# A filter layer by DFT products and a snake MLP in one kernel: a first stage folded on GpSimd for batches 3 to 7, and the sign of the filter put into its copy

## The chip, the core and the metric

The kernel runs on one core of a Trainium2 chip. The time is device time in microseconds, from several runs of one program; the profile is of one further execution. The engines are TensorE (PE, its weight loads shown as PEld), VectorE (DVE), ScalarE (ACT), GpSimd (POOL) and SyncE (SP, which here issues transfers only). TensorE writes to PSUM; ACT and DVE move results from there to SBUF.

## The reference

Two layers follow each other. The first multiplies the spectrum of `x` along the sequence by a filter; the second is an MLP with a snake activation.

```python
# x (8, 3008, 256); filt_r, filt_i (1505, 256)
X = np.fft.rfft(x, axis=1)
y = np.fft.irfft(X * (filt_r + 1j * filt_i)[None], n=3008, axis=1)
h = y.reshape(24064, 256) @ w_in              # (256, 2048)
s = np.sin(alpha * h)
g = h + s * s / (alpha + 1e-9)
out = g @ w_out                               # (2048, 256), float32
```

## The kernel before

The DFT of length 3008 = 47 x 64 is done in two stages of matrix products. The first (`first`, tile `pa`) is a DFT of length 47: 94 rows (47 positions, twice, for two halves of the 64 columns) against the table `wf_t`, 16 products of 512 columns a batch, each evacuated by `evac` into `t1_h` and stored four at a time to `d1` in DRAM. `load_t2` reads `d1` back with other rows (eight transfers on POOL's queue, two for each of four groups `t2[g]`). `forward` (`pb`, 12 a batch) is the second stage. `product` and `cross` multiply by the filter on DVE; for `cross`, SP swaps the two halves of `xf` into `xs`. `inverse` (`pc`) and `last` (`pd`) go back, by way of `d2` in DRAM and `load_t4` (tile `t_a`), and leave the rows in `y`. Batch 0 has functions of its own, with names ending in `_0`.

The MLP takes `y` in 48 chunks of 512 columns (the sixth of each twelve has 384). `hidden` makes 128 of the 2048 hidden rows (two products `ph`), ACT takes a sine of it, DVE forms the activation `v` with one operation on `cos_all` (SBUF) and `ph` (PSUM); `project` multiplies by `w_out` (`po`), ACT copies the result to `o`, and `store` issues it, on POOL's queue for chunks below 5, and on SP's after.

The order of the work is written out by hand. The main loop goes through 8 steps a chunk; a step has two `hidden`, a `slot`, one or more `project`, and another `slot`. Work of the filter layer stands in the list `pending`, put there with a place in steps (`put`); `slot(at)` takes from it what is due, at most one piece with TensorE work unless one is over a step late. For a batch b the places count from z = 48 b. Before, in batches 3 to 7, `load_x` stands at z - 92 + 7 ch, `first` at z - 67 + 0.66 i, `load_t2` at z - 56, `forward` from z - 46.8 every 2.3 steps, `product` and `cross` 1.5 and 4.5 steps after it, `inverse` 6 after, `load_t4` at z - 10.5 and z - 3. Each engine works through its own instructions in this order, and so do the queues that SP and POOL issue. On SP stand the stores to `d1` and `d2`, the swaps, `load_t4`, and from chunk 5 the stores of `o`.

The filter's two parts lie in `f_t[0]` and `f_t[1]`, each wanted in both halves of the partitions. `other_half` copies one half into the other; `negate`, at steps 13 and 14, turns the sign of half of `f_t[1]` in place. Batch 0 works before that, and has the missing sign in its own table, `e1_0`, through the vector `sign`.

Of the kernel before, what the change touches and what calls it, by code (L numbers as in the profile page):

```python
# [22 lines left out]
NR = 2 * N1  # L23
NK = 4 * NS
FUSED = 1


def dft_tables():

    n1, n2 = np.arange(N1), np.arange(N2)  # L30
    s, q = np.arange(NS), np.arange(NQ)
    ph = 2 * np.pi * np.outer(n1, s) / N1
    w = np.stack([np.cos(ph), -np.sin(ph)], 1)
    wf = np.zeros((N1, 2, 2, NS, 2))
# [12 lines left out]
    d[0, :, :, 0] = c.transpose(0, 2, 1)
    d[1, :, :, 0] = sn.transpose(0, 2, 1)
    d[0, :, :, 1] = (-sn * sg).transpose(0, 2, 1)
    d[1, :, :, 1] = (c * sg).transpose(0, 2, 1)  # L50
    f16 = np.float16
    wf, wi = wf.reshape(N1 * 2, 2, NS, 2), 2 * wi.reshape(2, NS, 2, NR)
    wf0, wi0 = np.zeros((96, 2, 2, 32)), np.zeros((2, 2, 32, NR))
    wf0[:NR, :, :, :NS] = wf.transpose(0, 1, 3, 2)
    wi0[:, :, :NS] = wi.transpose(0, 2, 1, 3)
    d = d.reshape(128, NS, 128).astype(f16)
    e = d.transpose(2, 1, 0) * f16(0.125)
    return (wf.reshape(NR, NK).astype(f16), wi.reshape(NK, NR).astype(f16), d,
            wf0.reshape(96, 128).astype(f16), wi0.reshape(128, NR).astype(f16), e)


# [1 line left out]
def kernel(  # L63
# [8 lines left out]
    out: bass.AP,  # L72
):
    nc = tc.nc
    wf_host, wi_host, d_host, wf0_host, wi0_host, e_host = dft_tables()
    wf_dram = nc.inline_tensor(wf_host, name="wf_tbl")
    wi_dram = nc.inline_tensor(wi_host, name="wi_tbl")
    d_dram = nc.inline_tensor(d_host, name="d_tbl")
    wf0_dram = nc.inline_tensor(wf0_host, name="wf0_tbl")
    wi0_dram = nc.inline_tensor(wi0_host, name="wi0_tbl")  # L80
# [13 lines left out]
        return ctx.enter_context(tc.tile_pool(name=name, bufs=bufs, **kw))  # L94

    cpool = pool("consts", 1)
    xpool = pool("xp", 4)
    t2pool = pool("t2", 4)
    xfpool = pool("xf", 3)
    ppool = pool("pp", 4)  # L100
# [7 lines left out]
    ops = pool("ops", 2, PSUM)  # L108

    wf_t = cpool.tile([NR, NK], FP16)  # L110
    t1_h = [cpool.tile([128, 16, C], FP16, name=f"t1_h{i}") for i in range(2)]
    t4_a = cpool.tile([128, 2, 16, C], FP16)
    t4_h = [t4_a[:, i] for i in range(2)]

    def by_half(t):

        return t.rearrange("p a (b c) -> p (a b) c", c=128)

    cos_all = cpool.tile([128, 4, 512], FP32)
    y = cpool.tile([128, 2, 2, 32, NR], FP16)  # L120
# [15 lines left out]
    marks = {}  # L136

    def load_x(b, ch):
        xt = xpool.tile([NR, 8, C], FP16, name=f"x_{b}_{ch}", tag="x")
        for n0, n in [(0, 8)] if b or ch < 3 else [(0, 4), (4, 4)]:  # L140
            ins = nc.gpsimd.dma_start(  # L141
                out=xt[:, n0:n0 + n],
                in_=bass.AP(tensor=x.tensor, offset=x.offset + (b * S + ch * 8 + n0) * C,
                            ap=[[32 * C, NR], [C, n], [1, C]]),
            )
        if b == 0:
            marks["x", ch] = ins
        if b == 1:
            marks["x1", ch] = ins
            after(ins, marks["w_out"])  # L150
        if b > 1:
            after(ins, marks["snake"])
        return xt
# [3 lines left out]
    def evac(dst, src, on_act=None):  # L157
# [3 lines left out]
        else:  # L161
            marks["dve"] = nc.vector.tensor_copy(out=dst, in_=src)  # L162

    class Spectral:

        def __init__(self, b):
            self.b = b
            self.d1 = dpool.tile([2 * NS, N2, C], FP16, name=f"d1_{b}", tag="d1")
            self.d2 = dpool.tile([2 * NS, N2, C], FP16, name=f"d2_{b}", tag="d2")
            self.d1_rows = self.d1.rearrange("a (h n) c -> (a h) n c", h=2)  # L170
            self.d2_rows = self.d2.rearrange("a (h n) c -> (a h) n c", h=2)
            self.x, self.t2, self.t4, self.xf, self.xs, self.p = {}, {}, {}, {}, {}, {}
            self.fused = b >= FUSED

        def load_x(self, ch):
# [2 lines left out]
        def first(self, i):  # L178
            ch, j = divmod(i, 4)
            ps = fps.tile([128, 512], FP32, name=f"pa_{self.b}_{i}", tag="f")  # L180
            marks["pe"] = nc.tensor.matmul(out=ps[0:NK, :], lhsT=wf_t, rhs=self.x[ch][:, 2 * j:2 * j + 2, :],  # L181
                                           start=True, stop=True)
            r0 = 8 * (ch % 2)
            evac(t1_h[ch // 2][0:NK, r0 + 2 * j:r0 + 2 * j + 2, :], ps[0:NK, :])
            if j == 3:
                nc.sync.dma_start(out=self.d1_rows[:, 8 * ch:8 * ch + 8, :], 
                                  in_=t1_h[ch // 2][0:NK, r0:r0 + 8, :])

        def load_t2(self, g):
            self.t2[g] = t2pool.tile([128, 6, C], FP16, name=f"t2_{self.b}_{g}", tag="t2")  # L190
# [73 lines left out]
    id32 = cpool.tile([16, 16], FP32)  # L264
    nc.scalar.dma_start(out=id32, in_=id32_dram.ap())

    x0 = [xpool.tile([NR, 8, C], FP16, name="x_0_0", tag="x")] + [load_x(0, ch) for ch in range(1, 4)]
    nc.gpsimd.dma_start(out=d_t, in_=d_dram.ap())
    id16 = cpool.tile([128, 128], FP16)
    nc.gpsimd.dma_start(out=id16, in_=id16_dram.ap())  # L270
# [86 lines left out]
        nc.tensor.transpose(out=ps[:, 0:16], in_=rec, identity=id32)  # L357
        nc.vector.tensor_scalar(out=rec_t, in0=ps[:, 0:16], scalar1=-0.5, scalar2=None, op0=ALU.mult)

    sign = cpool.tile([128, 1], FP32)  # L360
    nc.vector.memset(sign[0:64], 0.125)
    nc.vector.memset(sign[64:128], -0.125)

    def inverse_table(g):

        gs = slice(8 * g, 8 * g + 8)
        ps = ops.tile([128, 8, 128], FP16, name=f"pse_{g}", tag="o")
        for i in range(8):
            for a in range(2):
                nc.tensor.transpose(out=ps[64 * a:64 * a + 64, i, :],  # L370
                                    in_=d_t[:, 8 * g + i, 64 - 64 * a:128 - 64 * a], identity=id16)
        nc.scalar.mul(e1_0[:, gs, :], ps, sign)

    warmed = []

# [7 lines left out]
    def other_half(g, k, on_act):  # L383

        gs = slice(12 * g, 12 * g + 12)
        evac(f_t[k][64 - 64 * k:128 - 64 * k, gs, :], f_t[k][64 * k:64 * k + 64, gs, :], on_act)

    warm_pe(10)
    def cast_x0(h):
# [47 lines left out]

    def product_0(i):
        hc, w = blocks[i]
        p0[i] = xpool.tile([128, 2, 4, 128], FP16, name=f"p_0_{i}", tag="x")  # L440
        marks["products"] = nc.vector.tensor_tensor(
            out=p0[i].rearrange("p f s (k c) -> p f s k c", k=2),
            in0=xf0[i].rearrange("p s (k c) -> p s k c", k=2)[:, None].to_broadcast([128, 2, 4, 2, 64]),
            in1=filt_t[:, :, 4 * w:4 * w + 4].rearrange("p f s (k c) -> p f s k c", k=2)[..., 64 * hc:64 * hc + 64],
            op=ALU.mult)
# [24 lines left out]
            after(ins, marks["filt", 1, 0])  # L470
    nc.sync.dma_start(out=wf_t, in_=wf_dram.ap())
    nc.sync.dma_start(out=wi_t, in_=wi_dram.ap())
    w_out32 = vpool.tile([128, 16, C], FP32, name="w_out32", tag="v")
    for jb in range(0, 16, 8):
        ins = nc.sync.dma_start(out=w_out32[:, jb:jb + 8],
# [121 lines left out]
    for jb in range(12, 16):  # L597
        put(5 + 0.5 * (jb - 12), weights_out, jb, 1)

    def negate(i):  # L600

        gs = slice(12 * i, 12 * i + 12)
        nc.vector.tensor_scalar(out=f_t[1][0:64, gs, :], in0=f_t[1][0:64, gs, :],
                                scalar1=-1.0, scalar2=None, op0=ALU.mult)

    for i in range(2):
        put(13 + i, negate, i)
    for n0, n, at in ((6, 5, 1.5), (11, 4, 12.5), (15, 4, 14), (19, 4, 15.5), (23, 4, 17), (27, 5, 19)):
        put(at, last_0, n0, n, fps, "f", True)
    for b in range(1, B):  # L610
        s = s1 if b == 1 else Spectral(b)
        z = 48 * b
        if b > 1:
            for ch in range(4):
                put((22,27,32,37)[ch] if b == 2 else z - 92 + 7 * ch, s.load_x, ch)
        for i in range(16):
            put(6.9 + 0.35 * i if b == 1 else 36 + 0.66 * i if b == 2 else z - 67 + 0.66 * i, s.first, i, pe=True)
        for g in range(4):
            put(12.5 if b == 1 else max(z - 56, 46.5), s.load_t2, g)
        for u in range(12):  # L620
            inv = 23.5 + 1.25 * u if b == 1 else 59 + 2.1 * u if b == 2 else z - 40.8 + 2.3 * u
            fwd = inv - (6 if b == 1 else 6)
            put(fwd, s.forward, u, pe=True)
            put(fwd + (0.5 if b == 1 else 1.5), s.product, u)
            if s.fused:
                put(fwd + (4 if b == 1 else 4.5), s.cross, u)
            put(inv, s.inverse, u, pe=True)
        for ch in range(4):
            put(z - (9.5 if b == 1 and ch < 3 else (10.5, 10.5, 10.5, 3)[ch]), s.load_t4, ch)
        for u in range(16):  # L630
            put(z + (u - (5 if b == 1 else 6.5) if u < 4 else 2 * u - 9), s.last, u, pe=True)
# [59 lines left out]
```

## Time and profile before

| what | value |
|---|---|
| median of 3 runs | 785.87 us (785.68 to 786.81) |
| the profiled execution: its time, its span | 785.97 us, 784.2 us |
| granted TensorE clock | 0.999 |
| first-stage products (line 181) | 112 of 94x512, 42.4 us of pipelined busy time |
| activation on DVE (line 546) | 704 of 128x512, 682 ns each |
| transfers, share of 16 engines | hardware queue q1 33.4%, software queue q0 (POOL) 19.4% |

Busy time is the time in which an engine has at least one instruction under way. Matmuls overlap, so their lengths add to more than the time that they take; what one costs is read from the distance of starts. A line in a table of groups gives the source line, the engine, what is written and read, the shape, how often, the busy time, and the mean length; after the second bar stands the engine's idle time just ahead of these instructions, with what ended it. The span begins with the program's first instruction and ends with its last.

### The profile page before, as it was taken

What the parts mean: (1) busy time and instruction counts of PE and PEld (TensorE: products, weight loads), DVE (VectorE), ACT (ScalarE), POOL (GpSimd) and SP (SyncE); (2) the same over time, 40 slices, a digit from 0 to 9 for tenths busy, and PEclk for the clock granted to TensorE, in tenths of its full rate; (3) what the DMA queues carried; (4) which work ended last, traced back from release to release, by engine and by line L of the source; (5) the groups of instructions that cost most, each with busy time, mean ns of one, the idle gap of its engine ahead of it and who ended that gap; (6) DMA issues with size and microseconds to landing.
All of it is one profiled execution on the core that took longest, in us unless ns stands there. A gap on an engine that the chain in (4) does not pass through costs nothing.

```text
span 784.2 us, 16646 instructions
## 1 busy us (share of the span) xinstructions
PE 771.1 (98%) x5799; PEld 535.2 (68%) x5799; DVE 655.7 (84%) x1169; ACT 617.6 (79%) x1211; POOL 113.3 (14%) x190
## 2 busy tenths in 40 slices
PE   7999999999999999999999999999999999999998
PEld 4757766676667766777666766767667776766666
DVE  7897996899878997799877998799977999777773
ACT  5797987888878887888877887788887887777674
POOL 6456443500020000200020000200002000000000
PEclk9999999999999999999999999999999999999999
DMA  9956577755564546654575454835556243421112
GB/s 214 281 112 164 124 142 213 158 124 121 163 174 89 129 105 190 148 122 108 131 202 114 103 115 131 226 87 118 119 161 176 65 98 80 117 61 29 41 41 54
DMA packets 86655, 100.99 MB, mean 129 GB/s; under 512 B 14896, under 2 KB 74294, under 8 KB 86572
## 3 DMA queue, kind: packets, MB, share of 16 engines
q1 hardware_dynamic: 74644, 71.11, 33.4%
q0 software_dynamic: 11712, 28.78, 19.4%
q8 instruction: 45, 0.74, 0.4%
q14 instruction: 38, 0.31, 0.1%
q10 hardware_dynamic: 216, 0.05, 0.0%
HBM read 55.72 MB, written 46.66 MB: 131 GB/s over the span
## 4 chain that ended last, share of the span: by engine, by line
PE 92%; DVE 3%; DMA 1%; ACT 1%; issue 1%; SPq 0%; ACTq 0%; DVEq 0%
PE po L558 40%; PE ph L541 39%; PE pa L181 3%; PE pd L254 2%; PE pb L201 2%; PE pc L232 2%; DVE v L546 2%; PE pc L453 1%; DMA al<-in_moe_alpha_dram 1%; ACT cos_all L545 1%; PE warm L381 1%; PE pb L431 1%; DMA t_a<-d 0%; SPq L586 0%; PE pa L399 0%
## 5 line engine op out<-in xcount | busy, mean ns | idle before, releaser
L546 DVE SCALAR_TENSOR_TENSOR v<-cos_all,ph 128x512 f16<-128x512 f32 (+1 forms) x768 | 482.9, 671 | 106.8 <-ACT cos_all L545 103.6
L545 ACT ACTIVATE cos_all<-ph 128x512 f32<-128x512 f32 (+1 forms) x768 | 411.2, 592 | 95.3 <-PE ph L541 94.3
L558 PE MATMUL po<-w,v 128*128 128x256 f16 x3008 | 389.5, 272 | 0.0
L541 PE MATMUL ph<-y,w 128*128 128x512 f16 (+1 forms) x1536 | 387.8, 374 | 1.6 <-DVE y L162 0.9
L558 PEld LDWEIGHTS <-v 128*128 128x128 f16 x3008 | 288.3, 98 | 78.3 <-issue 2.0
L541 PEld LDWEIGHTS <-w 128*128 128x128 f16 x1536 | 147.9, 98 | 103.9 <-issue 3.1
L566 ACT COPY o<-po 128x512 f32<-128x512 f32 (+1 forms) x97 | 55.6, 573 | 19.9 <-PE po L558 13.5
L586 POOL DMA_DIRECT2D out_dram<-o x67 | 35.0, 529 | 207.6 <-ACT o L566 205.4
L193 POOL DMA_DIRECT2D t<-d x56 | 36.3, 664 | 180.4 <-DMA out_dram<-o 98.7
L204 ACT CAST xf<-pb 128x512 f16<-128x512 f32 x84 | 50.0, 595 | 13.1 <-PE pb L201 12.3
L141 POOL DMA_DIRECT2D x<-in_x_dram x32 | 17.1, 537 | 259.7 <-PE pc L232 146.5
L160 ACT CAST t_h<-pa 96x512 f16<-96x512 f32 x74 | 43.3, 585 | 8.8 <-PE pa L181 8.5
L160 ACT CAST y<-pd 128x376 f16<-128x376 f32 (+1 forms) x82 | 39.5, 482 | 8.8 <-PE pd L254 5.3
L254 PEld LDWEIGHTS <-t_a 96*128 96x128 f16 x448 | 31.3, 97 | 19.8 <-DMA t_a<-d 1.4
L181 PE MATMUL pa<-x,wf_t 94*96 94x512 f16 x112 | 42.4, 381 | 0.6 <-ACT t_h L160 0.4
L160 ACT CAST g<-pc 128x512 f16<-128x512 f32 x61 | 36.2, 593 | 8.2 <-PE pc L232 7.8
L254 PE MATMUL pd<-wi_t,t_a 96*128 96x94 f16 x448 | 37.1, 204 | 1.1 <-DMA t_a<-d 1.1
L222 DVE TENSOR_TENSOR p<-p,xs 128x512 f16<-128x512 f16 x84 | 35.7, 425 | 2.9
L221 DVE TENSOR_TENSOR xs<-xs,filt_t 128x512 f16<-128x512 f16 x84 | 35.0, 417 | 0.0
L215 DVE TENSOR_TENSOR p<-xf,filt_t 128x512 f16<-128x512 f16 x84 | 35.0, 417 | 0.0
L201 PE MATMUL pb<-t,d_t 128*128 128x256 f16 x168 | 32.1, 272 | 0.2
L232 PE MATMUL pc<-p,e_t 128*128 128x256 f16 x168 | 32.1, 272 | 0.0
(66 smaller groups left out, 285.8 us busy)
## 6 DMA issues: line engine op xcount, KB each, us to landing
x<-in_x_dram POOLq DMA_DIRECT2D x30, 376.0 KB, 5.0
d<-t_h SPq DMA_DIRECT2D x28, 384.0 KB
t<-d POOLq DMA_DIRECT2D x56, 192.0 KB, 4.7
xs<-xf SPq DMA_DIRECT2D x168, 64.0 KB
d<-g SPq DMA_DIRECT2D x56, 192.0 KB
t_a<-d SPq DMA_DIRECT2D x28, 384.0 KB
out_dram<-o SPq DMA_DIRECT2D x92, 80.0 KB
w_out<-in_moe_w_out_dram SPq DMA_DIRECT2D x2, 1024.0 KB
```

What stands on the lines that cost most here:

```text
L160: marks["act"] = nc.scalar.copy(out=dst, in_=src)
L181: marks["pe"] = nc.tensor.matmul(out=ps[0:NK, :], lhsT=wf_t, rhs=self.x[ch][:, 2 * j:2 * j + 2, :], start=True, stop=True)
L193: nc.gpsimd.dma_start(out=self.t2[g][64 * p:64 * p + 64, :, :], in_=self.d1[a0:a0 + 6, :, :].rearrange("s n c -> n s c"))
L201: nc.tensor.matmul(out=ps[:, i, :], lhsT=d_t[:, s, :], rhs=self.t2[s // 6][:, s % 6, :], start=True, stop=True)
L204: nc.scalar.copy(out=self.xf[u], in_=ps)
L232: nc.tensor.matmul(out=ps[:, i, :], lhsT=e_t[:, 2 * w + i, :], rhs=pt[:, i, :], start=(k == 0), stop=(k == len(pr) - 1))
L254: nc.tensor.matmul(out=psv[:, i, :], rhs=wi_t, start=True, stop=True, lhsT=t4_h[ch // 2][0:NK, n0 % 16 + i, cb * 128:cb * 128 + 128])
L541: nc.tensor.matmul(out=ps[:, 0:n], lhsT=w1[:, cb, jb * 128:jb * 128 + 128], rhs=y_cols[:, cb, c0:c0 + n], start=(cb == 0), stop=(cb == 1))
L545: nc.scalar.activation(out=cs[:, 0:n], in_=ps[:, 0:n], func=AFT.Sin, bias=float(np.pi / 2))
L546: marks["snake"] = nc.vector.scalar_tensor_tensor(out=v[k][:, jb, 0:n], in0=cs[:, 0:n], scalar=-1.0, in1=ps[:, 0:n], op0=ALU.add, op1=ALU. ...
L558: nc.tensor.matmul(out=pso[k][:, t % 2, :], lhsT=v[k][:, jb, 128 * t:128 * t + 128], rhs=w2[:, jb, :], start=(jb == 0), stop=(jb == 15))
L566: nc.scalar.copy(out=o[:, i0:t % 2 + 1, :], in_=pso[k][:, i0:t % 2 + 1, :])
```

## The change

The filter's sign: `other_half` multiplies by -1 where it copies `f_t[1]`, `negate` and `sign` go, and the table of batch 0 has one factor for all rows. Batch 2: `load_x` at 22, 26, 30, 34 (before 22, 27, 32, 37), `first` from 37 every 0.63 steps, `load_t2` at 47.

Batches 3 to 7 get another first stage. A row n1 of the 47 and its mirror 47 - n1 have the same cosine and opposite sines, so their sum and their difference are transformed instead, over 24 rows. Five column groups of 13 go side by side (65 columns for 64; one is not used): 120 rows in, 120 out. `load_mirror` loads rows 1 to 23 and their mirrors with 15 transfers a batch on POOL's queue, `fold` makes sum and difference on GpSimd (two operations of 120x512 in seven pairs of columns, the last half as wide), and `first_folded` has two products for each pair, one against the cosines and one against the sines. The stores to `d1` are four a batch again, two after the fourth pair and two after the seventh. The folds of batch b start at z - 63.5 and the products at z - 61, both every 1.3 steps; `load_t2` stands at z - 50.8.

```diff
+FOLDED = 3
+NJ, NL = 5, 13
+NF = NJ * NS
...
+    even = np.cos(ph[:NS])
+    odd = -np.sin(ph[:NS])
+    wp = np.einsum("kis,jm->jiksm", np.stack([even, odd]), np.eye(NJ))
...
-    t1_h = [cpool.tile([128, 16, C], FP16, name=f"t1_h{i}") for i in range(2)]
+    t1_a = cpool.tile([128, 2, 16, C], FP16)
+    t1_h = [t1_a[:, i] for i in range(2)]
+    wp_t = cpool.tile([NF, 2, NF], FP16)
...
+    x_all = cpool.tile([128, 4, 8, C], FP16)
...
+    STORES = {3: 0, 6: 8}
+    NP = (NL + 1) // 2
+    x_rows = x_all.rearrange("p a n c -> p (a n) c")
+    mirror = [x_rows[:, 16 * k:16 * k + NL, :] for k in range(2)]
+    sums = [t[0:NF, NL:NL + 2, :] for t in (t1_h[0], t1_h[1], x_rows[:, 0:16], x_rows[:, 16:32])]
+
+    def start_folding():
+
+        nc.gpsimd.memset(mirror[1].bitcast(UINT32), 0)
...
+        def load_mirror(self, k, l0, n):
+            rows = [mirror[k][0:NF - NJ, l0:l0 + n]] + ([] if k or l0 else [mirror[k][NF - NJ:NF]])
+            for at, t in zip((N2 * (N1 - 1) if k else N2, 0), rows):
+                run = n if at else NL
+                ins = nc.gpsimd.dma_start(
+                    out=t, in_=bass.AP(tensor=x.tensor, offset=x.offset + (self.b * S + at - 1 + l0) * C,
+                                       ap=[[NL * C, NJ], [-N2 * C if k else N2 * C, NS - 1 if at else 1],
+                                           [1, run * C]]))
+                after(ins, marks["snake"])
+
+        def fold(self, i):
+            l0, n = 2 * i, min(2, NL - 2 * i)
+            xa, xb = [t[0:NF, l0:l0 + n, :] for t in mirror]
+            self.e[i] = sums[i % 4]
+            after(nc.gpsimd.tensor_tensor(out=self.e[i][:, 0:n, :], in0=xa, in1=xb, op=ALU.add), marks["snake"])
+            nc.gpsimd.tensor_tensor(out=xa, in0=xa, in1=xb, op=ALU.subtract)
+
+        def first_folded(self, i, k):
...
+            nc.tensor.matmul(out=dst, lhsT=wp_t[:, k, :], rhs=src, start=True, stop=True)
+            if n == 2:
+                evac(t1_a[0:NF, k, l0:l0 + 2, :], ps[0:NF])
+            elif k == 1:
+                evac(t1_a[0:NF, :, l0, :], ps[0:NF])
+            if i in STORES and k == 1:
+                lo = STORES[i]
+                n = l0 + n - lo
+                for part in range(2):
+                    nc.sync.dma_start(out=self.d1_fold[part, :, lo:lo + n, :], in_=t1_a[0:NF, part, lo:lo + n, :])
...
-        nc.scalar.mul(e1_0[:, gs, :], ps, sign)
+        nc.scalar.mul(e1_0[:, gs, :], ps, -0.125)
...
-        evac(f_t[k][64 - 64 * k:128 - 64 * k, gs, :], f_t[k][64 * k:64 * k + 64, gs, :], on_act)
+        if k == 0:
+            evac(f_t[0][64:128, gs, :], f_t[0][0:64, gs, :], on_act)
+        else:
+            nc.vector.tensor_scalar(out=f_t[1][0:64, gs, :], in0=f_t[1][64:128, gs, :],
+                                    scalar1=-1.0, scalar2=None, op0=ALU.mult)
...
     nc.sync.dma_start(out=wi_t, in_=wi_dram.ap())
+    nc.sync.dma_start(out=wp_t, in_=wp_dram.ap())
...
-        put(13 + i, negate, i)
...
+        if s.folded:
+            if b == FOLDED:
+                put(z - 94, start_folding)
+            for i in range(NP):
+                for k in range(2):
+                    put(z - 92 + 2.6 * i + 1.3 * k, s.load_mirror, k, 2 * i, min(2, NL - 2 * i))
+            for i in range(NP):
+                at = z - 61 + 1.3 * i
+                put(at - 2.5, s.fold, i)
+                for k in range(2):
+                    put(at + 0.7 * k, s.first_folded, i, k, pe=True)
+        else:
+            if b > 1:
+                for ch in range(4):
+                    put(22 + 4 * ch, s.load_x, ch)
+            for i in range(16):
+                put(6.9 + 0.35 * i if b == 1 else 37 + 0.63 * i, s.first, i, pe=True)
...
-            put(12.5 if b == 1 else max(z - 56, 46.5), s.load_t2, g)
+            put(12.5 if b == 1 else 47 if b == 2 else z - 50.8, s.load_t2, g)
```

More of the change, by code (lines that the diff above doesn't have):

```diff
@@ L57, in dft_tables @@
     e = d.transpose(2, 1, 0) * f16(0.125)
-    return (wf.reshape(NR, NK).astype(f16), wi.reshape(NK, NR).astype(f16), d,
+    even = np.cos(ph[:NS])
+    odd = -np.sin(ph[:NS])
+    wp = np.einsum("kis,jm->jiksm", np.stack([even, odd]), np.eye(NJ))
+    wp = np.concatenate([wp[:, 1:].reshape(NF - NJ, 2, NF), wp[:, 0].reshape(NJ, 2, NF)])
+    return (wp.astype(f16), wf.reshape(NR, NK).astype(f16), wi.reshape(NK, NR).astype(f16), d,
             wf0.reshape(96, 128).astype(f16), wi0.reshape(128, NR).astype(f16), e)
@@ L74 @@
     nc = tc.nc
-    wf_host, wi_host, d_host, wf0_host, wi0_host, e_host = dft_tables()
+    wp_host, wf_host, wi_host, d_host, wf0_host, wi0_host, e_host = dft_tables()
     wf_dram = nc.inline_tensor(wf_host, name="wf_tbl")
     wi_dram = nc.inline_tensor(wi_host, name="wi_tbl")
+    wp_dram = nc.inline_tensor(wp_host, name="wp_tbl")
     d_dram = nc.inline_tensor(d_host, name="d_tbl")
@@ L96 @@
     cpool = pool("consts", 1)
-    xpool = pool("xp", 4)
     t2pool = pool("t2", 4)
@@ L117, in by_half, with x_tile @@
         return t.rearrange("p a (b c) -> p (a b) c", c=128)
+    x_all = cpool.tile([128, 4, 8, C], FP16)
+    x_made = []
+    def x_tile():
+        x_made.append(x_all[:, len(x_made) % 4])
+        return x_made[-1]
     cos_all = cpool.tile([128, 4, 512], FP32)
@@ L138, in load_x @@
     def load_x(b, ch):
-        xt = xpool.tile([NR, 8, C], FP16, name=f"x_{b}_{ch}", tag="x")
+        xt = x_tile()[0:NR]
         for n0, n in [(0, 8)] if b or ch < 3 else [(0, 4), (4, 4)]:
@@ L167, in __init__ @@
             self.b = b
-            self.d1 = dpool.tile([2 * NS, N2, C], FP16, name=f"d1_{b}", tag="d1")
+            self.folded = b >= FOLDED
+            if self.folded:
+                self.d1_all = dpool.tile([2 * NS, NJ * NL, C], FP16, name=f"d1_{b}", tag="d1f")
+                self.d1 = self.d1_all[:, 1:1 + N2, :]
+                self.d1_fold = self.d1_all.rearrange("(k s) (j l) c -> k (s j) l c", k=2, j=NJ)
+            else:
+                self.d1 = dpool.tile([2 * NS, N2, C], FP16, name=f"d1_{b}", tag="d1")
+                self.d1_rows = self.d1.rearrange("a (h n) c -> (a h) n c", h=2)
             self.d2 = dpool.tile([2 * NS, N2, C], FP16, name=f"d2_{b}", tag="d2")
-            self.d1_rows = self.d1.rearrange("a (h n) c -> (a h) n c", h=2)
             self.d2_rows = self.d2.rearrange("a (h n) c -> (a h) n c", h=2)
-            self.x, self.t2, self.t4, self.xf, self.xs, self.p = {}, {}, {}, {}, {}, {}
+            self.e, self.x, self.t2, self.t4, self.xf, self.xs, self.p = {}, {}, {}, {}, {}, {}, {}
             self.fused = b >= FUSED
@@ L187, in first @@
                                   in_=t1_h[ch // 2][0:NK, r0:r0 + 8, :])
+        def load_mirror(self, k, l0, n):
[14 more added lines that the diff above has]
+        def first_folded(self, i, k):
+            l0, n = 2 * i, min(2, NL - 2 * i)
+            if n == 2 or k == 0:
+                self.ps1 = fps.tile([128, 2, C], FP32, name=f"pa_{self.b}_{i}_{k}", tag="f")
+            ps = self.ps1
+            if k == 0:
+                src = self.e[i][:, 0:n, :]
+            else:
+                src = mirror[0][0:NF, l0:l0 + n, :]
+            dst = ps[0:NF, 0:2, :] if n == 2 else ps[0:NF, k:k + 1, :]
+            nc.tensor.matmul(out=dst, lhsT=wp_t[:, k, :], rhs=src, start=True, stop=True)
[8 more added lines that the diff above has]
+                    nc.sync.dma_start(out=self.d1_fold[part, :, lo:lo + n, :], in_=t1_a[0:NF, part, lo:lo + n, :])
         def load_t2(self, g):
@@ L265 @@
     nc.scalar.dma_start(out=id32, in_=id32_dram.ap())
-    x0 = [xpool.tile([NR, 8, C], FP16, name="x_0_0", tag="x")] + [load_x(0, ch) for ch in range(1, 4)]
+    x0 = [x_tile()[0:NR]] + [load_x(0, ch) for ch in range(1, 4)]
     nc.gpsimd.dma_start(out=d_t, in_=d_dram.ap())
@@ L358, in reciprocals @@
         nc.vector.tensor_scalar(out=rec_t, in0=ps[:, 0:16], scalar1=-0.5, scalar2=None, op0=ALU.mult)
-    sign = cpool.tile([128, 1], FP32)
-    nc.vector.memset(sign[0:64], 0.125)
-    nc.vector.memset(sign[64:128], -0.125)
     def inverse_table(g):
@@ L385, in other_half @@
         gs = slice(12 * g, 12 * g + 12)
-        evac(f_t[k][64 - 64 * k:128 - 64 * k, gs, :], f_t[k][64 * k:64 * k + 64, gs, :], on_act)
+        if k == 0:
+            evac(f_t[0][64:128, gs, :], f_t[0][0:64, gs, :], on_act)
+        else:
+            nc.vector.tensor_scalar(out=f_t[1][0:64, gs, :], in0=f_t[1][64:128, gs, :],
+                                    scalar1=-1.0, scalar2=None, op0=ALU.mult)
     warm_pe(10)
@@ L439, in product_0 @@
         hc, w = blocks[i]
-        p0[i] = xpool.tile([128, 2, 4, 128], FP16, name=f"p_0_{i}", tag="x")
+        p0[i] = x_tile()[:, 0:4].rearrange("p n (f c) -> p (n f) c", f=2).rearrange("p (f s) c -> p f s c", f=2)
         marks["products"] = nc.vector.tensor_tensor(
@@ L598 @@
         put(5 + 0.5 * (jb - 12), weights_out, jb, 1)
[L600 to L606, printed above, removed]
-        put(13 + i, negate, i)
     for n0, n, at in ((6, 5, 1.5), (11, 4, 12.5), (15, 4, 14), (19, 4, 15.5), (23, 4, 17), (27, 5, 19)):
@@ L612 @@
         z = 48 * b
[L613 to L617, printed above, removed]
+        if s.folded:
[9 more added lines that the diff above has]
+                    put(at + 0.7 * k, s.first_folded, i, k, pe=True)
+        else:
+            if b > 1:
[3 more added lines that the diff above has]
+                put(6.9 + 0.35 * i if b == 1 else 37 + 0.63 * i, s.first, i, pe=True)
         for g in range(4):
-            put(12.5 if b == 1 else max(z - 56, 46.5), s.load_t2, g)
+            put(12.5 if b == 1 else 47 if b == 2 else z - 50.8, s.load_t2, g)
         for u in range(12):
```

## The prediction

> **What bounds the kernel now.** I read the page's busy times first, then the table by stretches, then the waits, then the timeline around one batch's first stage.
>
> ```profile
> PE 771.1 (98%) x5799; PEld 535.2 (68%) x5799; DVE 655.7 (84%) x1169; ACT 617.6 (79%) x1211; POOL 113.3 (14%) x190
> ...
> PE   7999999999999999999999999999999999999998
> ```
>
> From the third slice of 40 on, TensorE (PE) has no idle time. That alone proves little, since matmul ends are modelled, so I take its pace from starts in the timeline (start us, length, engine, line):
>
> ```profile
> 306.31 0.38 PE L181 MATMUL pa<-x,wf_t 94*96 94x512 f16 x1
> ...
> 320.44 1.89 PE L541 MATMUL ph<-y,w 128*128 128x512 f16 x8
> 322.17 0.33 PE L254 MATMUL pd<-wi_t,t_a 96*128 96x94 f16 x4
> 322.34 1.04 PE L558 MATMUL po<-w,v 128*128 128x256 f16 x8
> 323.22 0.38 PE L201 MATMUL pb<-t,d_t 128*128 128x256 f16 x2
> ```
>
> Eight 512-column matmuls take 322.17 - 320.44 = 1.73 us, 0.216 each; four of 94 columns take 0.17; eight of 256 take 0.88, 0.110 each (384 columns by the same reading: 0.163). The 272 to 381 ns of the groups are pipelined lengths, not costs. Adding these paces over the program's PE order gives 87.9 us from batch 2's first `pb` to batch 3's; the trace has 142.65 to 230.66, 88.0. So PE runs at its pace without gaps: a column removed there is gained whole, and a stall put there is paid whole.
>
> **The change, part by part.**
>
> *PE columns (gain, whole).* Before, a batch has 16 `pa` products of 512 columns: 16 x 0.216 = 3.46 us. After, six of the seven pairs give two of 512 and the last two of 256: 12 x 0.216 + 2 x 0.110 = 2.81. Rows rise from 94 to 120, which no row here charges for (94- and 128-row matmuls of equal width keep one pace). Five batches: 5 x 0.65 = **-3.2 us**. The evacuations fall from 16 to 13 per batch (582 ns on ACT, 680 on DVE): both engines have idle time, so nothing.
>
> *Sign in the copy.* Two in-place negations go; the copy of `filt_i` becomes a multiply of the same shape (946 against 956 ns, nothing).
>
> ```profile
> L603 DVE TENSOR_SCALAR filt_t<-filt_t x2: 945/946/946, 61.4 to 64.0; 64x3072 f16<-64x3072 f16 x2
> ```
>
> The second, at 64.01, stands ahead of two casts of `y`; the later cast ends at 67.07 and PE waits for it:
>
> ```profile
> 67.12 0.38 PE L541 MATMUL ph<-y,w 128*128 128x512 f16 x1 [0.90 <-DVE y L162]
> ```
>
> Without 0.95 us ahead of it that wait should go: **-0.9** (0 to -1.3, with the 0.34 at 64.99).
>
> *Batch 2's loads.* One PE wait of 1.1 us stands in the list for `t_a` at about 125, while `x` from step 37 (113.6 us, 7.1 to land against some 4.9 for its neighbours) is in flight. That load moves to step 34: **-0.5** (0 to -1.1). Against it, `load_t2` of batch 2 moves on POOL's queue behind eight stores of `o` (eight x 0.53 = 4.2 us after the copy that ends at 134.1, so to about 138.4, where the first load started at 136.87): pair landed at 138.4 + 4.3 = 142.7 against a `pb` at 142.65: **+0.3** (0 to +1.5).
>
> *Table and memset.* `wp_t` is one more issue on SP, 0.35 us like its neighbours, ahead of `w_out`; cover is POOL's scaling of `w_in` until 43.2; without it 0.35. The memset (some 1.6 us by 271 ns for 128 and 170 for 16 columns) and 15 mirror loads per batch instead of 4 (11 x 0.6 us) lie on a POOL that is idle for tens of microseconds; nobody waits for them before the fold, 11 steps after the last.
>
> *The folds on GpSimd.* Float16 sums of 120x512 aren't in the trace. Nearest rows:
>
> ```profile
> L482 POOL TENSOR_TENSOR w<-w_in,y 128x768 f16<-128x768 f32 x4 | 7.3, 1825 | 13.1 <-DVE rec_t L358 13.1
> ...
> L514 POOL TENSOR_TENSOR w<-w_out,rec_t 128x1024 f16<-128x1024 f32 x3 | 5.6, 1896 | 0.0
> ...
> L482 POOL TENSOR_TENSOR w<-w_in,y 128x512 f16<-128x512 f32 x2 | 2.6, 1279 | 0.0
> ```
>
> I take 1.28 us (same element count); bounds 0.42 (16x128, with less data) and 1.9 (1024 columns). A fold is a sum and a difference, 2.6 us; folds stand 1.3 steps apart, and with these products a step is some 2.2 us of PE pace, so 2.9: POOL keeps up. Its start waits for a DVE result some 2 us late, the product stands 2.5 steps (5.5 us) later: 5.5 - 2 - 1.3 = 2.2 us of slack. **0.** At 1.9 us a fold takes 3.8, lags 0.9 each, 5.4 over six, 3 us of it over the slack: 5 x 3 = 15 us. DVE beside GpSimd work:
>
> ```profile
> L546 DVE SCALAR_TENSOR_TENSOR v<-cos_all,ph 128x512 f16<-128x512 f32 x20 | 12.4, 680 | 1.8 <-ACT cos_all L545 1.8
> ```
>
> That is from 36 to 53 us, while POOL multiplies; 682 elsewhere. So the activation isn't slowed. [...]
>
> *The move, and what it makes late.* The first stage ends at z - 52.5 instead of z - 57.1, but `forward` still starts at z - 46.8. In the changed PE order, between the last `pa` and the first `pb` stand, in batches 3, 5, 7: 20 x 0.216 + 40 x 0.110 + 3 x 0.17 = 9.2 us (before 19.4); in batches 4, 6: 12 x 0.163 + 8 x 0.216 + 32 x 0.110 + 3 x 0.17 = 7.7 (before 16.8). In that time must pass: evacuation, the `d1` store by SP, its landing, POOL's two loads of `t2[0]`, their landing. The same chain in batch 4 of before:
>
> ```profile
> 307.71 0.30 SPq L186 DMA_DIRECT2D d<-t_h  x1
> ```
> ```profile
> 312.91 5.21 POOL L193 DMA_DIRECT2D t<-d  x8 [32.57 <-DMA out_dram<-o]
> ```
> ```profile
> L193 POOL DMA_DIRECT2D t<-d x2: 670/672/673, 312.9 to 313.6; - x2
> ...
> DMA to landing us min/median/max: 3.5/3.7/3.8
> ```
>
> Last product 306.31, store 307.71, first load 312.91, pair landed 313.57 + 3.8 = 317.4: 11.0 us. The same views give 9.4 and 9.2 us in batches 1 and 2, and 12.8, 11.0, 11.1, 10.9, 11.3 in batches 3 to 7. Before, all fitted in 16.8. After, neither space holds the usual 11. Which value? Batches 3 to 7 had three `t_a` loads (384 KB each) issued just ahead of the store (303.23 to 304.86 in batch 4); now these are some 13 us earlier, which favours the short rows; but the last store grows from 384 to 600 KB in two DMAs, and six stores of `o` (four in the odd batches) now stand ahead of it on SP at 0.38 us each: in batches 4 and 6 they free SP 1.7 us after the product, where an evacuation takes 1.4. I take 9.9 us, 10.2 in 4 and 6. Counting the last product itself (0.1), stalls are 9.9 - 9.35 = 0.55 three times and 10.2 - 7.83 = 2.4 twice: **+6.4 us**. Bounds: 9.2 gives 0 and 1.4, +2.8; 12.8 gives 3.45 and 5.0, +20. Behind the waiting `pb` stand the next batch's `ph` and `po` in PE's order, and ACT and DVE wait for those; nothing makes it up later, since PE has no idle time to give. Behind the waiting store on SP stand the fourth `t_a` load, needed a dozen steps on, and stores; behind the waiting `t2` load on POOL only mirror loads.
>
> [...]
>
> **The sum**, against the profiled span: 784.2 - 3.2 - 0.9 - 0.5 + 0.3 + 6.4 = 786.3. The profiled run took 785.97, 1.8 beyond its span, and the median of the runs is 785.87, so I carry the difference: 785.9 + 2.1 = **788.0 us**.
>
> **Rivals.**
> 1. *The chain is as short as in batches 1 and 2, or shorter* (for: the `t_a` loads are gone from before it, the store's halves land separately; against: the larger store, `o` in the queue). At 9.2 the stalls are 2.8, and -4.3 + 2.8 = -1.5: 784.4. At 8.5 they are 2 x 0.7: 785.9 - 4.3 + 1.4 = 783.0. It is faster as soon as the stalls are under 2.7 us.
> 2. *GpSimd becomes the bound* at 1.9 us an operation, 15 us more: some 803. For: no float16 row, and each difference waits for its sum. Against: the 1279 ns row. It decides from 1.6 us.
> 3. *DMA queues as full as before*: chain 11.1, stalls 3 x 1.75 + 2 x 3.3 = 11.9: 793.5. It shares the forecast's mechanism.
>
> **Chances.** Forecast and rival 3 together 0.47 (0.42 slower, 0.05 within), rival 1 0.43 (0.28 faster, 0.15 within), rival 2 and the like 0.10, slower. A measurement of this kernel tells 0.2% (1.6 us) from no change. Faster 0.28, within 0.20, slower 0.52. The likeliest's own range is 786 to 791; with both signs open the range is 782 to 795, leaving the GpSimd bound and the worst of the loaded chain outside.
>
> **What would show it.** In the changed profile: PE idle before `pb`, released by the DMA of `t2`, some 2.4 us in batches 4 and 6, about half a microsecond in 3, 5, 7; no PE wait for POOL before `pa`; no 0.9 us wait near 67; POOL operations near 1.3 us; store to first `t2` load about 4 us. I am wrong if `pb` starts on time in 4 and 6, or if `pa` waits for POOL.

## The result, and the profile after

| | before | changed |
|---|---|---|
| median, lowest and highest of six runs | 786.37 us (785.68 to 787.22) | 791.71 us (790.56 to 795.25) |
| ratio of the times, 95% interval | | 1.0073 (1.0056 to 1.0090) |
| the profiled execution: its time, its span | 785.97 us, 784.2 us | 792.46 us, 790.5 us |

The kernel became slower by some 5.3 us. The changed runs lie 4.7 us apart, those of before 1.5.

From the page of the changed kernel: busy time of each engine, TensorE's busy share and its clock in 40 slices, and the folds' row (count, then busy us and mean ns, then the idle time before them).

```profile
PE 771.7 (98%) x5789; PEld 533.8 (68%) x5789; DVE 651.9 (82%) x1160; ACT 612.7 (78%) x1201; POOL 227.2 (29%) x316
...
PE   8999999999999999899999999999998999999998
...
PEclk9999999999999999999999999999999999999999
...
L236 POOL TENSOR_TENSOR t_a<-x_all 120x512 f16<-120x512 f16 x20 | 23.1, 1154 | 111.7 <-DVE v L618 111.7
```

GpSimd's work doubled, but it stands idle for 111.7 us ahead of these folds: POOL waits to be released, and no wait for POOL is in TensorE's list. TensorE's slices, full from the third on before, now have two dips inside the run, in the 17th and the 31st. (Slices of 20 us are too coarse for the clock, as the window table below shows.) The list of waits (what waited, for what; us in all, times, longest) has a row that the kernel before lacks:

```profile
PE pb L272 <- DMA t<-d: 7.5, 4, 2.7
...
PE ph L613 <- DVE y L179: 0.8, 1, 0.8
```

Four first `pb` products wait for `t2[0]`: 0.99 us in batch 2, then 2.08, 1.69 and 2.71 in batches 4, 6 and 7, which makes the 7.5. The wait for `y` near 67 us, forecast to go, is still there. Around the first stage of batch 4, TensorE's timeline (start us, length, engine, line; in brackets the idle time and its end) and those of SP and POOL:

```profile
313.98 0.28 PE L249 MATMUL pa<-x_all,wp_t 120*120 120x256 f16 x1
...
320.90 1.04 PE L630 MATMUL po<-w,v 128*128 128x256 f16 x8
324.01 0.39 PE L272 MATMUL pb<-t,d_t 128*128 128x256 f16 x2 [2.08 <-DMA t<-d]
```

```profile
313.33 2.08 SPq L658 DMA_DIRECT2D out_dram<-o  x5
315.51 0.83 SPq L258 DMA_DIRECT2D d<-t_a  x2
```

```profile
318.65 5.42 POOL L264 DMA_DIRECT2D t<-d  x8 [9.47 <-DMA d<-t_a]
```

Read them as one chain: last `pa` at 313.98, the `d1` store at 315.51 behind five stores of `o`, the first `t2` load at 318.65, `pb` at 324.01. From `pa` to `pb` there are 10.03 us, where the work between them fills 7.83 by the forecast's paces: 2.2 lost. The same subtraction gives:

| batch | 3 | 4 | 5 | 6 | 7 | sum |
|---|---|---|---|---|---|---|
| space without a wait (from the forecast) | 9.35 | 7.83 | 9.35 | 7.83 | 9.35 | |
| last `pa` to first `pb`, changed kernel | 9.51 | 10.03 | 9.52 | 9.82 | 12.18 | |
| lost | 0.16 | 2.2 | 0.17 | 2.0 | 2.8 | 7.4 |
| idle time at that `pb` | 0.04 | 2.08 | 0.05 | 1.69 | 2.71 | 6.6 |

The last two rows differ because the work between the two products takes up to 0.3 us more than the forecast's paces say. Batch 2's wait, 0.99 us, is in neither sum. One more loss shows only in the table by stretches (PE, PEld, DVE, ACT and POOL busy us with instructions, then the granted clock, the DMA share and GB/s), after the wait in batch 7, which ended at 608.57:

```profile
604.00:608.57 4.57, 1.87 (x16) 1.17 (x15) 2.41 (x5) 1.08 (x2) 3.72 (x6) 1.00 0.84 229
608.57:612.00 3.43, 3.43 (x16) 2.00 (x17) 1.28 (x2) 1.57 (x3) 0.00 (x0) 0.68 0.93 254
612.00:616.00 4.00, 4.00 (x29) 2.71 (x28) 1.80 (x4) 3.25 (x7) 0.00 (x0) 0.85 0.05 13
```

After 2.71 us of idle the clock falls to half for 3.41 us, from 609.8. In this trace 512-column products start 0.215 us apart from 608.79, and 0.427 apart from 611.21: work takes twice as long, so half of the 3.41, an estimated 1.7 us, is lost as well.

The span's +6.3 us: TensorE is ready for batch 2's first `pb` 2.0 us earlier (140.70 in place of 142.65), the wait there takes 1.0 back, the saved columns give 3.2 (worked out, not measured in this trace), waits in batches 3 to 7 cost 7.4, the slow clock 1.7. That makes +4.9; some 1.4 us, small waits among it, I have not assigned.

### The profile page after: what moved, and what is told of

It reads as the page before. It is cut to its first block, busy times and chain, and to the rows that moved or that the text cites. A ratio compares the mean times of both kernels' runs of the same rounds, so it can differ in the third digit from the quotient of the medians.

```text
span 790.5 us, 16825 instructions
## 1 busy us (share of the span) xinstructions
PE 771.7 (98%) x5789; PEld 533.8 (68%) x5789; DVE 651.9 (82%) x1160; ACT 612.7 (78%) x1201; POOL 227.2 (29%) x316
## 4 chain that ended last, share of the span: by engine, by line
PE 86%; DMA 6%; DVE 5%; ACT 2%; issue 1%; POOL 0%; ACTq 0%; SPq 0%; DVEq 0%; POOLq 0%
PE po L630 38%; PE ph L613 36%; DVE v L618 3%; PE pb L272 2%; PE pc L303 2%; DMA t<-d 2%; PE pd L325 2%; PE pa L249 2%; DMA d<-t_a 1%; DMA xs<-xf 1%; PE pa L214 1%; ACT cos_all L617 1%; DMA out_dram<-o 1%; PE pc L524 1%; DMA al<-in_moe_alpha_dram 1%
## 5 line engine op out<-in xcount | busy, mean ns | idle before, releaser
L226 POOL DMA_DIRECT2D x_all<-in_x_dram x75 | 47.6, 636 | 147.9 <-DVE v L618 141.8
L236 POOL TENSOR_TENSOR t_a<-x_all 120x512 f16<-120x512 f16 x20 | 23.1, 1154 | 111.7 <-DVE v L618 111.7
L177 ACT CAST t_a<-pa 120x512 f16<-120x512 f32 (+1 forms) x63 | 37.2, 591 | 9.5 <-PE pa L249 5.2
L237 POOL TENSOR_TENSOR x_all<-x_all 120x512 f16<-120x512 f16 (+1 forms) x35 | 38.0, 1087 | 2.7
```

The source lines that it names most:

```text
L177: marks["act"] = nc.scalar.copy(out=dst, in_=src)
L226: ins = nc.gpsimd.dma_start(out=t, in_=bass.AP(tensor=x.tensor, offset=x.offset + (self.b * S + at - 1 + l0) * C, ap=[[NL * C, NJ], [-N2 * ...
L237: nc.gpsimd.tensor_tensor(out=xa, in0=xa, in1=xb, op=ALU.subtract)
```

## The experiments

My theory is the forecast's: columns are saved, and more than that is lost because the first stage ends later while `forward` stays. The rivals: GpSimd's work slows something, or the loss lies in batch 2 and the front. "Before" in each result is the kernel before, run on the same chip.

### Only the places, in the kernel before

```diff
-put(... else z - 67 + 0.66 * i, s.first, i, pe=True)
+put(... else z - 61 + 0.5666 * i, s.first, i, pe=True)
-    put(12.5 if b == 1 else max(z - 56, 46.5), s.load_t2, g)
+    put(12.5 if b == 1 else 46.5 if b == 2 else z - 50.8, s.load_t2, g)
```

> The kernel before, with nothing of the change but the late places of batches 3 to 7: the 16 products of the first stage at z - 61 + 0.567 i (last near z - 52.5) and load_t2 at z - 50.8; no folds, no mirror loads, no sign, no new table. Stall theory: the space between last product and first pb falls to 9.4 us (3, 5, 7) and 7.9 us (4, 6), the chain takes 9.2 to 11, so pb waits some 2 us in 4 and 6 and 0 to 2 in the others; 786.4 + 4 to 9, about 793, and slower than the changed kernel by up to the 3.2 us of columns that it doesn't save. Rival (the folds or the mirror loads on GpSimd cost the time): the places alone cost nothing, 786.4 within 1 us.

Measured: 790.80 us (790.06 to 791.47) against 785.78, ratio 1.0062 (1.0049 to 1.0075): +5.0. Its list of waits:

```profile
PE pb L201 <- DMA t<-d: 3.0, 3, 2.0
...
PE pd L254 <- ACT t_h L160: 1.3, 2, 0.7
```

No fold, no table and no mirror load is in this kernel, and it pays the same kind of wait: 3.0 us for `t2[0]`, and 1.3 in waits of `pd` for evacuations, which also lie closer now. The time is at the low end of what was expected: only batch 6 waits 2.0 us, batches 4 and 5 wait 0.35 and 0.62. The later place alone costs about as much as the whole change, which also saves columns and so has lost more than this on the way.

### The changed kernel with the second stage later

```diff
-inv = ... else z - 40.8 + 2.3 * u
+inv = ... else z - 38.4 + 2.1 * u
```

> The changed kernel with forward, product, cross and inverse of batches 3 to 7 moved: inverse at z - 38.4 + 2.1 u in place of z - 40.8 + 2.3 u, so the first pb comes 2.4 steps later and the last inverse where it was. Space from last product to first pb 12.3 and 13.8 us. Stall theory: no wait at pb in 3 to 7, and the column gain shows: 786.4 - 3.2 - 1.0 (before batch 1's pb) + 1.1 (batch 2's wait) = 783.3, between 782.5 and 784.5. Rival (GpSimd): stays above 789.

Measured: 782.54 us (782.03 to 782.85) against 785.78, ratio 0.9958 (0.9946 to 0.9970). TensorE in batch 4:

```profile
311.40 0.27 PE L249 MATMUL pa<-x_all,wp_t 120*120 120x256 f16 x1
...
313.21 0.27 PE L249 MATMUL pa<-x_all,wp_t 120*120 120x256 f16 x1
...
325.51 0.38 PE L272 MATMUL pb<-t,d_t 128*128 128x256 f16 x2
```

The space is 12.3 us and no idle time stands before `pb`. In batches 3 to 7 the chains took 8.9 to 11.0 us in spaces of 12.3 to 13.8. Moving the consumer by 2.4 steps brings back 9.2 us of medians (791.71 - 782.54). In the two profiled executions it is 10.4 (spans of 790.5 and 780.1): 7.4 of waits, 1.7 of clock and 0.3 of batch 2's wait are 9.4 of it, and 1.0 is not assigned. This is the strongest evidence for the theory: the folds, the loads and the store's size are all unchanged.

### The changed kernel without its sums and differences

```diff
-            after(nc.gpsimd.tensor_tensor(out=self.e[i][:, 0:n, :], in0=xa, in1=xb, op=ALU.add), marks["snake"])
-            nc.gpsimd.tensor_tensor(out=xa, in0=xa, in1=xb, op=ALU.subtract)
...
-                src = self.e[i][:, 0:n, :]
+                src = mirror[1][0:NF, l0:l0 + n, :]
```

> The changed kernel without the GpSimd sums and differences: the cosine products read the mirrored rows and the sine products the rows as loaded, so the first stage of batches 3 to 7 isn't a DFT. Mirror loads, products, stores and places are the same. Stall theory: the waits at pb stay, 789 to 793. Rival (GpSimd work slows DVE or makes the products wait): falls to 783 to 786.

Measured: 791.60 us (788.20 to 792.79) against 785.78, ratio 1.0070 (1.0055 to 1.0084), the changed kernel's time. Its waits, and its clock by stretches (columns as above) after the wait in batch 4:

```profile
PE pb L270 <- DMA t<-d: 6.6, 5, 2.1
```

```profile
321.00:325.00 4.00, 1.85 (x18) 1.25 (x16) 2.85 (x5) 1.35 (x3) 3.83 (x7) 1.00 0.85 227
325.00:328.41 3.41, 3.41 (x14) 1.82 (x12) 1.38 (x2) 1.78 (x3) 0.17 (x1) 0.50 1.05 254
```

GpSimd's arithmetic costs nothing at these places. The half clock comes again, for the same 3.41 us, but in another batch.

### The first stage earlier, or later still

Two moves of folds, products and `load_t2` together, in opposite directions.

```diff
-                at = z - 61 + 1.3 * i
+                at = z - 63.5 + 1.3 * i
...
-put(12.5 if b == 1 else 47 if b == 2 else z - 50.8, s.load_t2, g)
+put(12.5 if b == 1 else 47 if b == 2 else z - 53.3, s.load_t2, g)
```

> The changed kernel with folds, products and load_t2 of batches 3 to 7 2.5 steps earlier (products at z - 63.5 + 1.3 i, first fold at z - 66, load_t2 at z - 53.3), forward where it was. The space before the first pb is 13.7 to 15.9 us, so no waits there; the first two folds now lie beside the last cross of the batch before (z - 67.3 and z - 65). Stall theory: as e4_forward, 782 to 783.5. Rival (folds beside operations with two SBUF inputs shut DVE out): a cross of 0.42 us lengthened by up to a fold operation, 1.15 us, twice a batch, and if PE waits for it up to 10 us more.

Measured: 793.56 us (793.42 to 793.81) against 786.0, ratio 1.0096 (1.0083 to 1.0109): no better, but for another reason, the rival's. Its waits:

```profile
PE pc L303 <- DVE p L293: 7.6, 8, 1.4
...
PE pb L272 <- DMA t<-d: 1.1, 1, 1.1
```

The waits for `t2[0]` are gone except batch 2's, and a new one has come: `pc` waits for DVE's sum `p`. The durations of the operation that makes `p` (ns: shortest, median, longest) tell why; here in this kernel:

```profile
L293 DVE TENSOR_TENSOR p<-p,xs x84: 424/425/1259, 81.0 to 671.8; 128x512 f16<-128x512 f16 x84
```

and in the changed kernel:

```profile
L293 DVE TENSOR_TENSOR p<-p,xs x84: 424/425/427, 79.9 to 670.3; 128x512 f16<-128x512 f16 x84
```

Where they get long, in this kernel's timelines of DVE and of POOL, batch 5's folds stand beside batch 4's last `cross`:

```profile
384.45 1.28 DVE L618 SCALAR_TENSOR_TENSOR v<-cos_all,ph 128x512 f16<-128x512 f32 x2
385.65 1.04 DVE L292 TENSOR_TENSOR xs<-xs,filt_t 128x512 f16<-128x512 f16 x1
386.72 1.25 DVE L293 TENSOR_TENSOR p<-p,xs 128x512 f16<-128x512 f16 x1
```

```profile
384.03 1.14 POOL L236 TENSOR_TENSOR t_a<-x_all 120x512 f16<-120x512 f16 x1 [16.75 <-DVE v L618]
385.25 1.15 POOL L237 TENSOR_TENSOR x_all<-x_all 120x512 f16<-120x512 f16 x1
386.36 1.33 POOL L236 TENSOR_TENSOR t_a<-x_all 120x512 f16<-120x512 f16 x1
```

Operations of 0.42 us on DVE took 1.04 and 1.25, about as long as one GpSimd operation (1.14 to 1.33 here). Both have two SBUF inputs, as the rival has it. The activation, with one input in PSUM, is not lengthened: two of them take 1.28 us at 384.45 with POOL busy, and as much in the changed kernel at 194.49 with POOL idle. So the folds' late place is what spares the changed kernel these waits. The span is 11.9 us above the one with `forward` later; TensorE's idle time after batch 2's first `pb` is 8.7 us more, and the rest is not assigned.

The other way, 1.5 steps later than in the changed kernel:

```diff
-                at = z - 61 + 1.3 * i
+                at = z - 59.5 + 1.3 * i
...
-put(12.5 if b == 1 else 47 if b == 2 else z - 50.8, s.load_t2, g)
+put(12.5 if b == 1 else 47 if b == 2 else z - 49.3, s.load_t2, g)
```

> The changed kernel with folds, products and load_t2 of batches 3 to 7 1.5 steps later still (products at z - 59.5 + 1.3 i, load_t2 at z - 49.3); the space from last product to first pb falls to 6.6 us (3, 5, 7) and 5.5 us (4, 6). Stall theory with a chain of 9.9: waits of 3.3 three times and 4.4 to 4.6 twice, some 19 us in place of 7.4: 791.7 + 11.7 = 803. If in addition every wait of over 3 us lets the granted clock fall to half for 3.4 us, 1.7 us more for each, up to 810, and the profile shows half clock after at least the waits of 4 and 6. If the clock falls only by chance, 803 and at most one or two such stretches.

Measured: 812.89 us (811.20 to 814.68) against 786.17, ratio 1.0348 (1.0332 to 1.0363). The waits for `t2[0]` sum to 18 us by the spaces (2.35, 4.6, 4.2, 4.3, 2.6); the list names 17.4:

```profile
PE pb L272 <- DMA t<-d: 17.4, 5, 4.5
```

That is less than the slowdown, and the time is above both forecasts, 803 and 810. More of it shows in the stretches around batch 4's wait:

```profile
325.00:329.40 4.40, 0.04 (x1) 0.00 (x0) 1.36 (x3) 0.00 (x0) 4.20 (x7) 0.78 0.83 216
329.40:334.20 4.80, 4.71 (x17) 2.44 (x18) 1.38 (x2) 1.78 (x3) 0.00 (x0) 0.50 0.88 186
```

The clock is at half for 6.83 us here (from 327.43, while `pb` still waits), and for 3.41 us at each of the waits in batches 5 to 7: 17.06 us in all. Of these, 2.8 us lie inside the waits in batches 4 and 6, where TensorE has nothing to do; half of the other 14.26, 7.1 us, is lost. With these, 784.2 - 3.2 + 18 + 7.1 = 806.1 of a span of 809.3. In this run an idle TensorE was paid for twice: 18 us as idle time and some 7.1 by the clock after it.

### TensorE kept busy through the waits

```diff
+            if u == 0 and b in (4, 6, 7):
+                for i in range(8):
+                    nc.tensor.matmul(out=ps, lhsT=d_t[:, 0, :], rhs=w2[:, 0:2, :], start=True, stop=True)
```

> The changed kernel with eight matmuls of 512 columns that nobody reads (1.73 us) ahead of the first pb of batches 4, 6 and 7, where it waits about 2 us; PE works through part of the wait. If PE's idle time of 2 us and more is what lets the clock fall to half for 3.4 us, the granted clock stays at 1.0 and runs of 792 to 795 are gone: 788 to 790, within 1.5 us of each other. Rival (the clock falls for another reason): spread and clock as for the changed kernel, 788 to 795.

Measured: 793.87 us (790.11 to 794.78) against 786.0, ratio 1.0091 (1.0075 to 1.0107). Half a miss: the clock stays up, as forecast (0.999 or 1.0 in each of the six runs, and no stretch of half clock in the profiled one, of 794.44 us), but the time is not lower and the spread not smaller. In batches 4 and 6 `t2[0]` landed only 11.5 and 11.1 us after the last `pa`, and `pb` still waits 1.88 and 1.33 us behind the filler; in batch 7 it landed after 9.9, and the filler itself holds `pb` up until 11.0. In the changed kernel's six runs the granted clock goes with the time: 1.0 and 0.999 in the two of 790.6 us, 0.998 in those of 790.96 and 792.46, 0.997 in those of 793.69 and 795.25. But here the runs are as far apart with the clock up, so waits that differ from execution to execution have a part in the spread too.

### The sign alone, and batch 2 alone

In the kernel before, the sign put into the copy as in the diff, nothing else:

```diff
-        nc.scalar.mul(e1_0[:, gs, :], ps, sign)
+        nc.scalar.mul(e1_0[:, gs, :], ps, -0.125)
...
+            nc.vector.tensor_scalar(out=f_t[1][0:64, gs, :], in0=f_t[1][64:128, gs, :],
+                                    scalar1=-1.0, scalar2=None, op0=ALU.mult)
...
-        put(13 + i, negate, i)
```

> The kernel before with the filter's sign put into its copy alone: no negations at steps 13 and 14. By the prediction the PE wait near 67 us for a cast of y goes: 785.8 - 0.9 = 784.9 (784.5 to 785.8). Rival (the wait is taken over by another one or made up before batch 2): no difference, 785.8.

Measured: 784.83 us (784.41 to 786.38) against 786.0, ratio 0.9988 (0.9979 to 0.9997): -1.2. The size is near the forecast's 0.9, the cause is not the forecast's. In this kernel's timeline of TensorE the wait for `y` is still there:

```profile
66.52 0.38 PE L541 MATMUL ph<-y,w 128*128 128x512 f16 x1 [0.83 <-DVE y L162]
```

Two other waits are gone, the 0.34 us at 64.99 and, unforeseen, the 1.1 us for `t_a` at 125, whose loads were issued at 119.18 and not at 121.33 as before.

In the kernel before, batch 2's places as in the change:

```diff
-                put((22,27,32,37)[ch] if b == 2 else z - 92 + 7 * ch, s.load_x, ch)
+                put(22 + 4 * ch if b == 2 else z - 92 + 7 * ch, s.load_x, ch)
...
-put(... else 36 + 0.66 * i if b == 2 else z - 67 + 0.66 * i, s.first, i, pe=True)
+put(... else 37 + 0.63 * i if b == 2 else z - 67 + 0.66 * i, s.first, i, pe=True)
-            put(12.5 if b == 1 else max(z - 56, 46.5), s.load_t2, g)
+            put(12.5 if b == 1 else max(z - 56, 47), s.load_t2, g)
```

> The kernel before with the places of batch 2 alone: x at 22 to 34, first at 37 + 0.63 i, load_t2 at 47. By the prediction: -0.5 for the earlier x load and +0.3 for load_t2 behind the eight stores of o, 785.8 within 0.5 us. By the waits seen in the changed kernel: 0.7 to 1.1 us of wait at batch 2's first pb, so 786.5 to 787.

Measured: 784.93 us (784.24 to 785.94) against 786.17, ratio 0.9982 (0.9973 to 0.9991): -1.2, below both forecasts. The `t_a` wait went here too, with its loads issued at 116.23. So both parts remove the same 1.1 us and can't be added. The wait at batch 2's first `pb` was 0.11 us here, 1.0 in the changed kernel with the same places; there the first `t2` load went out 6.3 us after the last `pa`, here 5.5. Why it went later there I have not settled.

### Batch 2's loads half a step earlier

```diff
-put(12.5 if b == 1 else 47 if b == 2 else z - 50.8, s.load_t2, g)
+put(12.5 if b == 1 else 46.5 if b == 2 else z - 50.8, s.load_t2, g)
```

> The changed kernel with load_t2 of batch 2 back at step 46.5, ahead of the eight stores of o on POOL's queue. Stall theory: the 1.0 us wait at batch 2's first pb goes, all else stays: about 1 us below the changed kernel, 789.5 to 791. Rival (the wait comes from the late last product of batch 2 and not from the stores): no difference.

Measured: 791.07 us (788.16 to 792.22) against 785.78, ratio 1.0063 (1.0050 to 1.0077). The edit did not act: `first`'s last item, at 46.45, comes late, `load_t2` sorts after it, and the same stores of `o` stand ahead on POOL; batch 2's wait stayed at 1.1. The run counts as a repeat of the changed kernel, with the half clock after batch 6's wait of 1.95 us. Its waits differ from the first profile's: the subtraction of the table gives 0, 1.6, 0.3, 2.2 and 0.9 us for batches 3 to 7, 5.0 in all, and batch 7, which lost 2.8 there, lost 0.9 here.

### The two repairs together

The later second stage of the second experiment, and for batch 2 the earlier places of the kernel before (its load of `x` stays early):

```diff
-put(6.9 + 0.35 * i if b == 1 else 37 + 0.63 * i, s.first, i, pe=True)
+put(6.9 + 0.35 * i if b == 1 else 36 + 0.66 * i, s.first, i, pe=True)
-put(12.5 if b == 1 else 47 if b == 2 else z - 50.8, s.load_t2, g)
+put(12.5 if b == 1 else 46.5 if b == 2 else z - 50.8, s.load_t2, g)
-inv = ... else z - 40.8 + 2.3 * u
+inv = ... else z - 38.4 + 2.1 * u
```

> The changed kernel with the later forward of e4_forward and, for batch 2, first at 36 + 0.66 i and load_t2 at 46.5 as in the kernel before, so that its loads stand ahead of the eight stores of o on POOL's queue (x of batch 2 stays at 22 to 34). Stall theory: the 0.7 us wait of e4_forward at batch 2's first pb goes: 782.5 - 0.7 = 781.8, no wait at any first pb. Rival (that wait is the later last product's, or is made up elsewhere): 782.5 again.

Measured: 781.93 us (781.72 to 782.85) against 786.0, ratio 0.9950 (0.9938 to 0.9962). No first `pb` waits in any batch, and TensorE's slices on its page are full again:

```profile
PE   8999999999999999999999999999999999999998
```

It beats both kernels: by 4.1 us the one before, and the changed one's median by 9.8 (on another chip, where the kernel before ran within 0.4 us of its time there).

## Why the prediction was right, and where its sizes were off

The forecast was 788.0 us, slower, and the time is 791.71: inside the range of 782 to 795, just outside the likeliest's own of 786 to 791. Its mechanism holds: the later place alone costs 5.0 us, and room behind the first stage brings 9.2 back.

- *Columns, -3.2.* Consistent with the runs: with both repairs the kernel is 2.9 us below the one with the sign alone (784.83 - 781.93); batch 2's early `x` is also in that. From batch 2's first `pb` to the end, where it has no part, the profiled executions take 641.4 and 638.4 us: 3.0, near the forecast, though `forward` stands elsewhere in the second.
- *Folds, 0.* Right. An operation took 1.15 us, not 1.28; leaving the arithmetic out changed nothing. Beside DVE the planned places cost next to nothing: of the changed kernel's 252 operations of `product` and `cross` in batches 1 to 7 only one was lengthened (0.94 us, at 197.59), while 2.5 steps earlier lengthened ones made most of 7.6 us of waits.
- *Stalls, +6.4.* Right in kind, in place and nearly in size: 7.4 in the profiled execution, 5.0 in the repeat's. Batches 3 and 5 lost 0.16 and 0.17 (forecast 0.55), 4 and 6 lost 2.2 and 2.0 (2.4), but batch 7 lost 2.8, where the same chain took 12.0 us. The delay of the store behind `o` on SP is there: in batch 4 the evacuation ended at 315.0, the store went out at 315.51. That batch 4's chain of 10.0 us came so near to the 10.2 is in part luck: from the store to the first load it took 3.1 us in place of the 4 forecast, and the loads took 4.5 to 4.8 us to land in place of the 3.5 to 3.8 of before.
- *Batch 2's loads, -0.5 and +0.3.* Both too small: the wait for `t_a` went whole, 1.1, and the late `load_t2` cost 1.0. The reason given for the first is not shown: by the forecast's own numbers that load of `x` had landed at 120.7, ahead of the wait at 125, and with the sign alone, where `x` is not moved, the wait went as well.
- *Sign, -0.9.* The reasoning of this step failed: the second negation was not what PE waited for near 67 us. The wait kept 0.83 of its 0.90 us without it. The gain, 1.2 us with the sign alone, came with the end of two other waits.
- *The clock.* A missing term: the forecast priced an idle PE at its idle time alone. Each drop of 3.41 us under work cost an estimated 1.7 us more, and batch 7's was in the profiled execution.

Against the profiled execution the sum lacks 1.0 of stalls, 0.7 of batch 2's `t2`, 1.7 of clock, and the unassigned 1.4; larger early gains stand against them. Of the rivals, the short chain (9.2) was wrong in batches 4, 6 and 7, and GpSimd as the bound was far off. Full queues gave 793.5, nearer to 791.71 than the forecast; its stalls of 11.9 overshot, and that its sum came near is luck, since it too had no term for the clock.

## What to carry to other kernels

When a stage is shortened or put later, look at what stands between it and its consumer: from the last product through its evacuation, a store to DRAM and a dependent load it took 9.4 to 12.0 us in batches 3 to 7 of the changed kernel, and in two of them the space had shrunk from 16.8 to 7.8. Move the consumer rather than the producer when the producer's earlier place is shared: later `forward` won 9.2 us, earlier folds nothing, since beside them `cross` operations of 0.42 us on DVE took up to 1.38. Keep TensorE's idle stretches short: here one of 1.95 us (batch 6 of the repeat) was followed by 3.41 us of half clock, an estimated 1.7 us more, and one of 2.08 (batch 4 of the changed kernel) was not, as the next section shows.

## What the runs showed of the hardware

The granted clock fell to 0.5 for 3.41 us, or twice that, after single idle stretches of PE of 1.95 us (batch 6, in the repeat), 2.15 (batch 4, without the folds), 2.71 (batch 7, changed kernel), and 2.48 and more in the latest placing. It didn't after others as long: 2.08 (batch 4, changed kernel), 2.02 (batch 6, places alone), 2.21 (batch 3, latest placing).

The traces show what tells them apart. Within each of these executions the clock changes only at times that lie whole multiples of 3.413 us apart: in the changed kernel at 5.64, 609.80, 613.21 and 790.70 us, which is 177, 178 and 230 of these steps after the first; in the latest placing from 6.58 to 327.43 there are 94, from 327.43 to 429.83 there are 30. Cut the span into pieces at these times, and what goes with the clock here is TensorE's idle time inside one piece, not the length of the stretch:

| kernel, batch | idle stretch, us | of it inside one piece | clock in the next piece |
|---|---|---|---|
| changed, 4 | 2.08 | 1.14, then 0.94 | full |
| places alone, 6 | 2.02 | 1.27 | full |
| latest placing, 3 | 2.21 | 1.79 | full |
| without sums, 7 | 1.87 | 1.87 | full |
| repeat of the changed, 6 | 1.95 | 1.95 | half |
| without sums, 4 | 2.15 | 2.15 | half |
| changed, 7 | 2.71 | 2.19 | half |
| latest placing, 7 | 2.48 | 2.48 | half |
| latest placing, 4 | 4.46 | 2.40, then 2.06 | half, twice |

Two of these pieces in the changed kernel, in batches 4 and 7 (columns as above: TensorE is busy for 2.27 and 1.23 us):

```profile
319.67:323.08 3.41, 2.27 (x18) 1.32 (x16) 2.76 (x5) 2.09 (x5) 3.38 (x6) 1.00 0.86 223
606.39:609.80 3.41, 1.23 (x8) 0.75 (x9) 0.42 (x1) 0.81 (x2) 1.33 (x3) 1.00 1.02 302
```

In the twelve traces there are 2734 whole pieces from the first rise of the clock on. Every one with 1.95 us of idle time or more is followed by half clock, and none with 1.87 or less is. A wait in batch 4 fell on two pieces in the changed kernel (2.08 us, full clock after it) and on one in the kernel without sums (2.15 us, half clock). This is read from traces; no run moved a wait against the pieces on purpose.
